# Head transfers in turn on one queue, a small fetch removed, shorter dataless matmuls, and late transfers by halves in a GEGLU kernel

## The chip, the core and the metric

The kernel runs on one core of a Trainium2 chip. The metric is device time in microseconds of that core, smaller is better; a kernel's time is the median of several executions. The engines are PE (TensorE; matmuls, and PEld for its weight loads), DVE (VectorE), ACT (ScalarE), POOL (GpSimd) and SP (SyncE). SP and ACT issue the transfers (DMAs) of this kernel, each on a queue of its own.

## The reference

```python
def setup_inputs():
    ...
    B, S, D, F = 32, 32, 1024, 3584
    return {
        "x": _w((lambda *s: _rng.normal(s) * 0.05)(B, S, D)),
        "w_gate": _w((lambda *s: _rng.normal(s) * 0.05)(D, F)),
        "w_up": _w((lambda *s: _rng.normal(s) * 0.05)(D, F)),
        "w_down": _w((lambda *s: _rng.normal(s) * 0.05)(F, D)),
    }

def reference(x, w_gate, w_up, w_down):
    return (_gelu(x @ w_gate) * (x @ w_up)) @ w_down
```

All tensors are bf16; `_gelu` is the tanh form.

## The kernel before

The 1024 tokens are two blocks of 512 (NB); D is 8 tiles of 128 (DT), F is 28 (FT). The kernel computes both layers with one level of a Winograd scheme: each product of 2 by 2 blocks takes seven block products in place of eight.

In the first layer the weights are the left matrix: a11 and a12 are the lower and upper four D tiles of `w_gate`, a21 and a22 those of `w_up`. The right matrix is x transposed: b11 and b21 are the lower and upper D tiles of token block 0, b12 and b22 those of block 1. t1 to t4 are sums of the b's (VectorE), s1 to s4 sums of the a's (mostly GpSimd). F runs in 14 chunks of two tiles (loop at L364).

Of the seven products, a12 times b21 needs no sums. For the first 24 F tiles it is done ahead, in the head of the kernel, and kept in fp32 (`ahead`). This is done in six groups of four F tiles (`group_ahead`, L293, `product_ahead`, L282); group i reads the tile `a12_ahead[i]` (a12a for groups 0 and 1, a12b for 2 to 5), which `load_ahead(i, k0, k1)` (L209) fills for the D tiles k0 to k1 of a12. These are "the kept gate rows".

Head of the kernel, L195 to L361, is ordered by hand (`manual_schedule`): each engine runs its instructions in the order of the code. x comes in two ways: for the first two D tiles of b21 as plain rows (`load_nat` into x_nat, L196), transposed on PE (`transposed`, L260) and copied by VectorE into b21; for all else by a transposing DMA (`load_xT`, L216). Before the first data, PE runs six dataless matmuls of 512 columns on a constant tile (NWARM, L255). PE then does group 0 for D tile 0 by halves of the tokens, the transposes of D tile 1, the rest of group 0's first two D tiles (matmuls of 256 columns), group 1's first two D tiles (L333, matmuls of 512 columns), the last two D tiles of both groups (L335), groups 2 to 4, the first product of chunk 0 (b11), and group 5.

The framework gives each transfer one of eight completion semaphores in turn. A transfer adds 16 to it when it has landed. A transfer that is given a semaphore whose earlier transfer may still be under way has to wait for that one's landing before it is issued.

Lines that the steps below touch: SP's first transfers at L203 to L243; ACT's three at L207 (the small fetch `probe`, 16 rows of 8 bytes that nothing reads), L223 (second x_nat) and L226 (group 1's first two D tiles); `gelu(ident...)` at L252, whose activation makes ACT load its table; the sums `t1` (L345, needs b11 and b12), `t2` (L351, needs b22), `b22r` (L352), `t3` (L354).

Of the kernel before, what the change touches and what calls it, by code (L numbers as in the profile page):

```python
# [8 lines left out]
ACT = mybir.ActivationFunctionType  # L9
# [4 lines left out]
def kernel(  # L14
# [20 lines left out]
    nc = tc.nc  # L35
    P = nc.NUM_PARTITIONS
    fp32 = mybir.dt.float32
    f32r = mybir.dt.float32r
    bf16 = mybir.dt.bfloat16
# [7 lines left out]
    NB = 512  # L47
    assert N == 2 * NB and D == 2 * NB and F % (4 * P) == 0
    DT, FT = D // P, F // P
    KD = DT // 2  # L50
# [4 lines left out]
    KQ = DT // 4  # L55
    HF = FT // 2
    MT = NB // P
    NWARM = 6
    KB = 4
    QF = HF // 2  # L60
    batches = [(0, KB), (KB, QF), (QF, QF + KB), (QF + KB, HF)]
# [2 lines left out]
    wg_r = w_gate.rearrange("(dt dp) f -> dp dt f", dp=P)  # L64
# [8 lines left out]
    xpool = one.enter_context(tc.tile_pool(name="x", bufs=1))  # L73
    ework = one.enter_context(tc.tile_pool(name="ework", bufs=2))
# [32 lines left out]
    def acc(tag):  # L107
        return ps1.tile([P, NB], fp32, name=f"ps{tag}", tag=tag, bufs=BANKS[tag])
# [18 lines left out]
    def alloc_w(ci, which):  # L127
        w_tiles[ci, which] = wpool.tile(
            [P, DT, FC * P], bf16, name=("wg", "wu")[which], tag=("wg", "wu")[which], bufs=(3, 2)[which]
        )  # L130

    def load_w(eng, ci, which, d0, d1):
        f0 = ci * FC * P
        src = (wg_r, wu_r)[which]
        eng.dma_start(out=w_tiles[ci, which][:, d0:d1, :], in_=src[:, d0:d1, f0 : f0 + FC * P])

    def load_w_all(ci, which):

        alloc_w(ci, which)
        if (ci, which) != (NCH - 1, 0):  # L140
            load_w(nc.sync, ci, which, 0, KD if which == 0 and a12_stays(ci) else DT)
            return


        for d0 in (0, KD):
            load_w(nc.sync, ci, which, d0, d0 + KD)

    def a12_stays(ci):
        return chunks[ci][-1] < 2 * KB
# [37 lines left out]
    ones_w = nc.const_aps.tensor(1.0, [P, P], bf16)  # L187
    ones_m = nc.const_aps.tensor(1.0, [P, NB], bf16)
    ident = xpool.tile([P, P], bf16, name="ident")
    make_identity(nc, ident)  # L190
    NB_P = NB // P
# [3 lines left out]
    with tc.manual_schedule():  # L195
        def load_nat(eng, dt, p0, p1):  # L196
            eng.dma_start(  # L197
                out=x_nat[:, p0:p1, dt * P : (dt + 1) * P],
                in_=xf[p0 * P : p1 * P, (KD + dt) * P : (KD + dt + 1) * P].rearrange("(b p) d -> p b d", p=P),
            )  # L200
# [1 line left out]
        assert KQ == 2  # L202
        load_nat(nc.sync, 0, 0, NB_P)  # L203


        probe = xpool.tile([P // 8, KQ, 2], bf16, name="probe")
        nc.scalar.dma_start(out=probe, in_=wg_r[::8, KD : KD + KQ, :2])  # L207

        def load_ahead(i, k0, k1, eng=nc.sync):  # L209
            f0 = i * KB  # L210
            eng.dma_start(
                out=a12_ahead[i][:, k0:k1, :],
                in_=wg_r[:, KD + k0 : KD + k1, f0 * P : (f0 + KB) * P],
            )

        def load_xT(nb, d0, d1):  # L216
            t = ((b11, b12), (b21, b22))[d0 // KD][nb]
            nc.sync.dma_start_transpose(
                out=t[:, d0 % KD : (d1 - 1) % KD + 1, :], in_=xf[nb * NB : (nb + 1) * NB, d0 * P : d1 * P]
            )  # L220

        load_ahead(0, 0, 1)
        load_nat(nc.scalar, 1, 0, NB_P)  # L223
        load_ahead(0, 1, 2)
        load_xT(0, KD + KQ, DT)
        load_ahead(1, 0, KQ, nc.scalar)  # L226
        a12_ahead += [spool.tile([P, KD, KB * P], bf16, name="a12b", tag=t) for t in ("s2", "s4", "s1", "s3")]
        for i in (0, 1):
            load_ahead(i, KQ, KD)
# [5 lines left out]
        load_halves(3)  # L235
        for which in (1, 0):
            load_w_all(0, which)
        load_ahead(4, 0, KD)
        load_xT(0, 0, KD)
        load_xT(1, 0, KD)  # L240
        load_ahead(5, 0, KD)
        load_xT(1, KD, DT)
        for which in (1, 0):  # L243
            load_w_all(1, which)

        def gelu(src, tag, bufs):
            h = ework.tile([P, NB], bf16, name=tag, tag=tag, bufs=bufs)[:, : src.shape[-1]]
            nc.scalar.activation(h, src, ACT.Gelu_apprx_tanh)  # L248
            return h


        gelu(ident[:, :1], "h0", 6)  # L252

        warm_ps = acc("A")
        for _ in range(NWARM):  # L255
            nc.tensor.matmul(warm_ps, lhsT=ones_w, rhs=ones_m, start=True, stop=True)

        tps = [[ps1.tile([P, HALF * P], bf16, name="tp", tag="A", bufs=BANKS["A"]) for _ in range(2)] for _ in range(KQ)]

        def transposed(dt):  # L260
            for half, tp in enumerate(tps[dt]):
                p0 = half * HALF
                for b in range(HALF):
                    nc.tensor.transpose(  # L264
                        tp[:, b * P : (b + 1) * P], x_nat[:, p0 + b, dt * P : (dt + 1) * P], ident
                    )
                nc.vector.tensor_copy(b21[:, dt, p0 * P : (p0 + HALF) * P], tp)

        transposed(0)

        def prod(ps, lhs, rhs, start):
            for k in range(KD):
                nc.tensor.matmul(  # L273
                    ps,
                    lhsT=lhs[:, k, :],
                    rhs=rhs[:, k, :],
                    start=(start and k == 0),
                    stop=(k == KD - 1),
                    skip_group_check=True,
                )  # L280
# [30 lines left out]
        def first_product(ft):  # L311
            psa = acc("A")
            prod(psa, quads(*chunk_of(ft))[0], b11, True)
            if ft < NAHEAD:
                return psa, gelu(added(ahead_at[ft], psa), "h0", 6)
            return psa, snap(psa, "sn1", 4)
# [34 lines left out]
        tt(t2, b22, t1, SUB)  # L351
        group_ahead(5, "CCAA", between=lambda: nc.scalar.copy(b22r, b22))  # L352
        begun = {ft: (psa, gelu(c, "h0", 6)) for ft, (psa, c) in begun.items()}
        tt(t3, b22, b12, SUB)  # L354
        next(chunk0)
# [8 lines left out]
        for ci in range(NCH):  # L364
# [8 lines left out]
            sn5, sn2, h1, h0 = [], [], [], []  # L373
# [17 lines left out]
            if fts[-1] < NAHEAD:  # L391
                h0 = first
# [226 lines left out]
```

## Time and profile before

| | us |
|---|---|
| median of 3 runs | 273.55 (273.33 to 275.83) |
| span of the profiled execution | 272.0 |
| PE busy | 267.1 (98%) |
| VectorE, ScalarE, GpSimd busy | 201.2, 116.1, 119.3 |
| data read, written | 31.72 MB, 2.10 MB |

The profile is one execution; the span runs from its first to its last instruction, and the time of a run also holds what lies around the span. Times in rows are microseconds from the span's start unless marked ns. A row such as `a<-b` names what is written and what is read; L284 is line 284 of the kernel. An engine followed by q (SPq, ACTq) is that engine's queue issuing a transfer: the length is that of the issue, not of the transfer.

PE's first stretch, in order of time (start, length, instruction, the idle time ahead of it and what ended it):

```profile
0.78 2.72 PE L256 MATMUL psA<-const-bfloat16-1.0 128*128 128x512 bf16 x6 [0.78 <-PEq L603]
...
3.30 0.62 PE L264 MATMUL tp<-ident,x_nat 128*128 128x128 bf16 x4
4.31 0.61 PE L284 MATMUL psC<-b,a12a 128*128 128x256 bf16 x2 [0.39 <-DMA a12a<-in_w_gate_dram]
```

### The profile page before, as it was taken

Reading aid. Unit: us, or ns where it says so; the run is one execution under the profiler, and the core shown is the slowest. Engines: PE = TensorE matmul, PEld = TensorE weight load, DVE = VectorE, ACT = ScalarE, POOL = GpSimd, SP = SyncE. Lnnn points to the kernel's source line nnn. Section 1 sums busy time; section 2 is a strip of 40 time slices with the busy share of each in tenths; the row PEclk is TensorE's granted clock in tenths of the full one; section 3 lists DMA queues with packets and bytes.
Section 4 is the critical chain, followed back from the end, with each engine's and each line's share of the span. In section 5 each row is a group of like instructions: output and inputs, shape, how many; then the busy total and the mean of one; then the engine's idle time right before and its main releaser. Section 6 shows DMA issues by size and latency. Waiting matters only on the chain.

```text
span 272.0 us, 3399 instructions
## 1 busy us (share of the span) xinstructions
PE 267.1 (98%) x1199; PEld 193.4 (71%) x1212; DVE 201.2 (74%) x205; ACT 116.1 (43%) x189; POOL 119.3 (44%) x60
## 2 busy tenths in 40 slices
PE   8999999999999999999999999999999999999995
PEld 4444776886787688688688687764458888888884
DVE  1448998886976876876787458569999999997721
ACT  2335865545644643645636535434000307770000
POOL 1090099976995994994995978000000000000000
PEclk9999999999999999999999999999999999999999
DMA  7999130504505505415234290005981437855111
GB/s 174 323 227 281 39 99 17 158 25 130 154 2 154 154 4 154 128 27 157 69 88 118 50 319 17 0 2 182 356 273 60 158 112 253 276 187 174 54 61 58
DMA packets 56048, 35.86 MB, mean 132 GB/s; under 512 B 9824, under 2 KB 56032, under 8 KB 56032
## 3 DMA queue, kind: packets, MB, share of 16 engines
q1 hardware_dynamic: 52736, 33.17, 42.6%
q10 hardware_dynamic: 3296, 2.49, 2.9%
q8 instruction: 9, 0.15, 0.2%
q14 instruction: 7, 0.06, 0.1%
HBM read 31.72 MB, written 2.10 MB: 124 GB/s over the span
## 4 chain that ended last, share of the span: by engine, by line
PE 97%; DMA 1%; issue 0%; SPq 0%; DVE 0%
PE psA L273 38%; PE psA L425 24%; PE psC L273 19%; PE psC L425 7%; PE psA L284 5%; PE psC L284 3%; PE psC L588 1%; DMA a12a<-in_w_gate_dram 1%; SPq L197 0%; PE tp L264 0%; DVE o_last L589 0%
## 5 line engine op out<-in xcount | busy, mean ns | idle before, releaser
L273 PE MATMUL psA<-t,s 128*128 128x512 f32 x224 | 57.2, 397 | 0.0
L248 ACT ACTIVATE h<-c 128x512 bf16<-128x512 f32 x56 | 34.6, 631 | 41.6 <-DVE c L303 41.6
L273 PEld LDWEIGHTS psA<-t,s 128*128 128x128 f32 x224 | 42.1, 188 | 9.5
L170 POOL TENSOR_TENSOR s<-wu 128x1024 fp32r<-128x1024 bf16 x13 | 28.8, 2215 | 32.9 <-DMA wu<-in_w_up_dram 27.9
L171 POOL TENSOR_TENSOR s<-s,wg 128x1024 fp32r<-128x1024 f32 x14 | 31.7, 2263 | 15.0 <-DVE s L170 14.0
L173 POOL TENSOR_TENSOR s<-wg,wu 128x1024 fp32r<-128x1024 bf16 x13 | 28.4, 2188 | 0.0
L273 PE MATMUL psA<-b,wg 128*128 128x512 bf16 x119 | 27.8, 379 | 0.6
L273 PE MATMUL psA<-t,a22r 128*128 128x512 f32 x112 | 27.9, 391 | 0.0
L273 PE MATMUL psC<-t,s 128*128 128x512 f32 x112 | 27.9, 391 | 0.0
L273 PE MATMUL psC<-b22r,s 128*128 128x512 f32 x112 | 27.6, 389 | 0.0
L303 DVE TENSOR_TENSOR c<-sn,psA 128x512 f32<-128x512 f32 x32 | 21.8, 682 | 6.7 <-PE psA L273 5.7
L308 ACT COPY sn<-psC 128x512 f32<-128x512 f32 x28 | 16.4, 590 | 20.9 <-PE psC L273 15.2
L273 PEld LDWEIGHTS psC<-t,s 128*128 128x128 f32 x112 | 21.0, 188 | 4.5
L273 PEld LDWEIGHTS psA<-t,a22r 128*128 128x128 f32 x112 | 21.0, 188 | 4.5
L273 PEld LDWEIGHTS psC<-b22r,s 128*128 128x128 f32 x112 | 21.0, 188 | 4.4
L303 DVE TENSOR_TENSOR c<-sn,psC 128x512 f32<-128x512 f32 x28 | 19.2, 688 | 6.5 <-PE psC L273 6.5
L273 PEld LDWEIGHTS <-wg 128*128 128x128 bf16 x128 | 11.8, 98 | 15.3 <-issue 2.4
L172 POOL TENSOR_TENSOR s<-wg,s 128x1024 fp32r<-128x1024 bf16 x10 | 21.6, 2158 | 0.8
L402 DVE TENSOR_TENSOR lo<-c,h 128x512 bf16<-128x512 f32 x14 | 20.4, 1459 | 0.9
L308 ACT COPY sn<-psA 128x512 f32<-128x512 f32 x32 | 18.4, 592 | 6.1 <-PE psA L273 6.0
L303 DVE TENSOR_TENSOR c<-ahead,psA 128x512 f32<-128x512 f32 x24 | 16.4, 687 | 4.0 <-PE psA L273 2.4
L321 DVE TENSOR_TENSOR hi<-h,psA 128x512 bf16<-128x512 bf16 x14 | 9.6, 688 | 12.4 <-PE psA L273 12.4
(85 smaller groups left out, 381.0 us busy)
## 6 DMA issues: line engine op xcount, KB each, us to landing
wu<-in_w_up_dram SPq DMA_DIRECT2D x14, 512.0 KB, 4.0
wdb<-in_w_down_dram SPq DMA_DIRECT2D x12, 512.0 KB, 4.9
wg<-in_w_gate_dram SPq DMA_DIRECT2D x9, 512.0 KB, 5.2
wdb<-in_w_down_dram SPq DMA_DIRECT2D x12, 384.0 KB, 4.5
v<-in_w_down_dram SPq DMA_DIRECT2D x4, 512.0 KB, 6.4
out_dram<-o_sb ACTq DMA_DIRECT2D x15, 128.0 KB, 1.7
wg<-in_w_gate_dram SPq DMA_DIRECT2D x6, 256.0 KB, 4.6
v<-in_w_down_dram SPq DMA_DIRECT2D x4, 384.0 KB, 7.5
```

Source lines behind the costliest of these rows:

```text
L170: yield engs[0].tensor_tensor(s1, a21, a22, ADD)
L171: yield engs[1].tensor_tensor(s2, s1, a11, SUB)
L172: yield engs[2].tensor_tensor(s4, a12, s2, SUB)
L173: yield engs[3].tensor_tensor(s3, a11, a21, SUB)
L248: nc.scalar.activation(h, src, ACT.Gelu_apprx_tanh)
L273: nc.tensor.matmul(ps, lhsT=lhs[:, k, :], rhs=rhs[:, k, :], start=(start and k == 0), stop=(k == KD - 1), skip_group_check=True,)
L284: nc.tensor.matmul(ps[:, cols], lhsT=a12_ahead[i][:, k, j * P : (j + 1) * P], rhs=b21[:, k, cols], start=(k == 0 and not cols.start), stop ...
L303: tt(t, s, ps, ADD)
L308: nc.scalar.copy(t, ps)
L321: tt(g_of(ft)[:, :NB], h0, psa, MUL)
L402: tt(g_of(ft)[:, NB:], added(sn5[fl], psa[fl]), h1[fl], MUL)
L425: nc.tensor.matmul(banks[m], lhsT=lhs(k)[:, m * P : (m + 1) * P], rhs=rhs(k), start=(start and k == 0), stop=(k == HF - 1), skip_group_che ...
```

## The change

- SP issues the head's first four transfers in turn: first x_nat, group 0's D tile 0, second x_nat (before on ACT's queue), group 0's D tile 1.
- The small fetch `probe` is gone.
- `gelu(ident...)`, with the table load, now stands ahead of ACT's one remaining transfer, group 1's first two D tiles.
- Five dataless matmuls in place of six, and two groups of two short ones (128 columns, `fill`): one ahead of the transposes of D tile 0, one behind them.
- The kept rows of groups 4 and 5 and the transposed loads of b11 and b12 go by halves (two D tiles) in turn; b22 goes by halves too, and chunk 1's gate rows stand ahead of b22, its up rows behind.

```diff
-    NWARM = 6
+    NWARM = 5
+    NFILL = 2
...
-        probe = xpool.tile([P // 8, KQ, 2], bf16, name="probe")
-        nc.scalar.dma_start(out=probe, in_=wg_r[::8, KD : KD + KQ, :2])
...
+        def gelu(src, tag, bufs):
+            h = ework.tile([P, NB], bf16, name=tag, tag=tag, bufs=bufs)[:, : src.shape[-1]]
+            nc.scalar.activation(h, src, ACT.Gelu_apprx_tanh)
+            return h
+
+
+        gelu(ident[:, :1], "h0", 6)
+
         load_ahead(0, 0, 1)
-        load_nat(nc.scalar, 1, 0, NB_P)
+        load_nat(nc.sync, 1, 0, NB_P)
         load_ahead(0, 1, 2)
+        load_ahead(1, 0, KQ, nc.scalar)
         load_xT(0, KD + KQ, DT)
-        load_ahead(1, 0, KQ, nc.scalar)
...
-        load_ahead(4, 0, KD)
-        load_xT(0, 0, KD)
-        load_xT(1, 0, KD)
-        load_ahead(5, 0, KD)
-        load_xT(1, KD, DT)
-        for which in (1, 0):
-            load_w_all(1, which)
-
-        def gelu(src, tag, bufs):
...
-        gelu(ident[:, :1], "h0", 6)
+        for i, nb in ((4, 0), (5, 1)):
+            for k in range(0, KD, KQ):
+                load_ahead(i, k, k + KQ)
+                load_xT(nb, k, k + KQ)
+        load_w_all(1, 0)
+        load_xT(1, KD, KD + KQ)
+        load_xT(1, KD + KQ, DT)
+        load_w_all(1, 1)
 
         warm_ps = acc("A")
         for _ in range(NWARM):
             nc.tensor.matmul(warm_ps, lhsT=ones_w, rhs=ones_m, start=True, stop=True)
+
+        def fill():
+            for _ in range(NFILL):
+                nc.tensor.matmul(warm_ps[:, :P], lhsT=ones_w, rhs=ones_w, start=True, stop=True)
+
+        fill()
...
         transposed(0)
+        fill()
```

The built programs differ in one more way that the diff does not spell out. These are ACT's first instructions with the semaphores they wait for, before and after:

```
L207 DMACopy probe<-in_w_gate_dram 16x2x2
L197 DMACopy x_nat<-in_x_dram 128x4x128
L211 DMACopy a12a<-in_w_gate_dram 128x2x512
L248 LoadActFuncSet
L248 Activation h0<-ident 128x1 [waits Pool]
```

```
L221 LoadActFuncSet
L221 Activation h0<-ident 128x1 [waits Pool]
L208 DMACopy a12a<-in_w_gate_dram 128x2x512 [waits DMAHW4 >= 16]
```

DMAHW4 is the semaphore that the first transposing DMA of x (b21's last two D tiles, on SP) raises by 16 when it has landed. ACT's load raises it by another 16, and PE's first weight load of group 1 waits for that.

More of the change, by code (lines that the diff above doesn't have):

```diff
@@ L237 @@
             load_w_all(0, which)
-        load_ahead(4, 0, KD)
-        load_xT(0, 0, KD)
-        load_xT(1, 0, KD)
-        load_ahead(5, 0, KD)
-        load_xT(1, KD, DT)
-        for which in (1, 0):
-            load_w_all(1, which)
-        def gelu(src, tag, bufs):
-            h = ework.tile([P, NB], bf16, name=tag, tag=tag, bufs=bufs)[:, : src.shape[-1]]
-            nc.scalar.activation(h, src, ACT.Gelu_apprx_tanh)
-            return h
-        gelu(ident[:, :1], "h0", 6)
+        for i, nb in ((4, 0), (5, 1)):
[6 more added lines that the diff above has]
+        load_w_all(1, 1)
         warm_ps = acc("A")
```

## The prediction

> **What bounds the kernel now.** I read the page's chain first: does any engine but PE carry it, and where does it leave PE?
>
> ```profile
> PE 97%; DMA 1%; issue 0%; SPq 0%; DVE 0%
> ```
>
> PE carries 97%, so what is not PE's own work is a few us. The same chain in order of time, for the first 60 us:
>
> ```profile
> 1.25 3.02 DMA a12a<-in_w_gate_dram
> ...
> 4.31 0.61 PE psC L284 x2
> 4.92 0.43 PE psA L284 x2
> ...
> 6.10 0.22 PE psA L284 x2
> ...
> 7.11 1.95 PE psA L284 x10
> ```
>
> The columns are start, length and what. PE's chain begins with the landing at 4.27 (1.25 + 3.02) of the first gate row tile, and from there PE follows PE to the end. So the end moves one for one with any time that PE loses or gains after 4.31. The row at 7.11 is where group 1 begins, the first product that reads gate tile a12a of the second group; I use it as the mark. The rows also show pace: two 256-column matmuls took 0.43 at 4.92 and 0.22 from 6.10. PE thus ran at half its later pace until about 6.0, 5.3 us after its first matmul at 0.78, although the granted clock in the rows stands at 1.00 throughout; the six dataless matmuls took 2.72.
>
> Next the two engines that issue the head's transfers, in order of time, SyncE and then ScalarE (start, length, instruction):
>
> ```profile
> 0.74 0.45 SPq L197 DMA_DIRECT2D x_nat<-in_x_dram  x1
> 1.25 1.03 SPq L211 DMA_DIRECT2D a12a<-in_w_gate_dram  x2
> 2.32 1.34 SPq L218 DMA_TRANSPOSE b<-in_x_dram  x1
> ...
> 19.21 3.65 SPq L218 DMA_TRANSPOSE b<-in_x_dram  x1
> ```
>
> ```profile
> 1.73 0.53 ACTq L211 DMA_DIRECT2D a12a<-in_w_gate_dram  x1
> 2.29 1.28 ACT L248 ACT_TABLE_LOAD   x1 [2.29 <-issue]
> 3.59 0.21 ACT L248 ACTIVATE h<-ident 128x1 bf16<-128x1 bf16 x1
> ```
>
> Issues on SP follow each other 0.51 apart (1.25 - 0.74). ScalarE issues group 1's first gate rows at 1.73, waiting for nothing. Last the DMA issues of these moments (size, us from issue to landing):
>
> ```profile
> x_nat<-in_x_dram SPq DMA_DIRECT2D x1, 128.0 KB, 2.5
> x_nat<-in_x_dram ACTq DMA_DIRECT2D x1, 128.0 KB, 3.2
> a12a<-in_w_gate_dram ACTq DMA_DIRECT2D x1, 256.0 KB, 4.6
> ```
>
> ```profile
> b<-in_x_dram SPq DMA_TRANSPOSE x1, 4.9
> ```
>
> Group 1's first rows landed at 1.73 + 4.6 = 6.3, 0.8 before their use at 7.11. The first transposed load of x (the one at 2.32) landed at 2.32 + 4.9 = 7.2.
>
> **The change part by part.**
>
> *The held load.* In the built program ScalarE's load of group 1's first gate rows now carries a wait: the semaphore that the first transposed load of x raises must have reached 16, that load's landing. Before, it had its own semaphore and no wait; the two loads share one now because ScalarE's turn comes after its table load and activation, when SP's transfers have gone once round the eight semaphores. So this load cannot be issued before x's transposed load has landed, and PE waits for it at the mark. Behind it in ScalarE's queue stand only the copies of finished groups, which need PE anyway.
>
> When does the transposed load land? SP issues one more transfer ahead of it, so it starts at 2.32 + 0.51 = 2.83 and, at 1.34, is issued by 4.17. Low end: the transposed load at 19.21 was issued by 22.86 and landed 5.7 after its start, at 24.9, that is 2.05 after its issue; 4.17 + 2.05 = 6.2. High end: the 4.9 of before from its start, 2.83 + 4.9 = 7.7. I take 6.6, nearer the low end: in the run of before 384 KB of ScalarE's transfers moved among SP's in these microseconds (128 KB landing at 4.4, 256 KB at 6.3), and these are gone from ahead of it.
>
> How long does the held load then take? Low end 2.5, the first x_nat, which had the DMA engines nearly to itself at half the size. High end 4.6, the same load of before, which stood behind 128 KB on its own queue. At its new time SP's queue is full: the windows show 344 to 352 GB/s from 7 to 10. ScalarE's 128 KB took 3.2 beside SP's loads; another 128 KB at half of 344 GB/s is 131/172 = 0.76, or 3.96; the faster engines of that later moment (344 against 203 to 232 GB/s at 2 to 4 us) take some off. I take 3.7.
>
> PE passes the mark at 6.6 + 0.1 + 3.7 = 10.4 in place of 7.11 (0.1 for the two hand-overs; PE began 0.05 after the landing at 4.27). That is 3.3 us later. Ends: 6.2 + 0.1 + 2.5 = 8.8, 1.7 later; 7.7 + 0.1 + 4.6 = 12.4, 5.3 later. Everything PE needs next (the later gate rows of groups 0 and 1, group 2) is issued on SP between 4.2 and 7 and takes 4.2 to 5.3 as before, so no second wait follows.
>
> *First four transfers on SP, no small fetch, shorter dataless matmuls.* Five long at 0.43 (2.15) and two short ones (a quarter of the columns, 0.11 each) end at 0.78 + 2.15 + 0.22 = 3.15, before the first x_nat (0.74 + 2.5 = 3.24). The two fills after the transposes take 0.22 while VectorE copies (its first copy ran from 3.75 to 4.04), so they delay nothing. Gate row 0 no longer shares the engines with ScalarE's transfers; it landed at 4.27 and PE can't start before the copy at 4.04: a gain of 0 to 0.26. Gate row 1 is issued at 2.27 in place of 1.76 and takes 2.5 to 4.4 (the row of before), landing at 4.8 to 6.7; PE waited 0.25 for it at 6.28: from a gain of 0.25 to a loss of 0.4. Together I take a gain of 0.4, and PE at the mark at 6.7. All of it is swallowed by the wait until 10.4; it counts only if the held load is in time. The dropped fetch frees 0.48 of ScalarE's issue time (0.73 to 1.21), also before the wait.
>
> *The clock behind the stall.* PE would stand from 6.7 to 10.4, 3.7 us. The longest PE idle that the trace shows after its start is below 1 us, so no row tells whether the pace halves again. Bounds: 0, or half of the 5.3 us of the first start, 2.65. That first start held some 1.3 us of waits (0.71 for x_nat, 0.39 and 0.25 for gate rows), so 4.0 busy us at half pace, a loss of 2.0, is what I take if it does.
>
> The Trainium skill speaks against the change here: by "TensorE: Matmul & The Clock Gate", Part 1, the half-rate state returns after an idle window of about 3.4 us, and a busy window lifts it. The trace agrees with the second half (half pace first, full pace from about 6.0) and shows nothing of the first. By that rule a 3.7 us gap would about suffice where the free-running window happens to fit into it, and an estimate from the page's window is 3.4/2 = 1.7 us lost.
>
> *Late kept rows and x's transposes by halves.* Six transposed halves and four gate halves replace three and two whole ones, same bytes. SP is 0.51 later there, and the held load's 256 KB (0.75 at 350 GB/s) now moves among them. First users in the run of before: group 4 at about 19.3, b11 at 22.7, group 5 at 24.4; landings then 15.9, 19.5 (10.30 + 9.2), 23.0 (17.34 + 5.7). Group 4's second half now stands behind one transposed half (256 KB, 0.9 at 290 GB/s): 15.9 + 0.5 + 0.75 + 0.9 = 18.1, in time. b12 stands behind group 5: from 21.2 to at most 21.2 + 0.5 + 0.75 + 1.5 = 24.0; VectorE's t1 and t2 (2.3 each) with two sums (1.5) between end at 30.1, where PE wanted t2 at 29.74. With PE 3.3 later that is hidden; without, it costs up to 0.4. The second chunk's up rows swap places with gate rows: landed 27.3, wanted at 32.98. Nothing.
>
> The sum: 0 + 3.3 + 0 = 3.3. The profiled span is 272.0; 1.55 lie around it up to the median of 273.55. So 275.3 in the span and 276.85 in time.
>
> **The rivals.**
>
> *The clock closes in the stall.* The 2.0 come on top: 278.85. For it: the first start; against: the gap is short. The span from 6.7 to 10.4 may also just miss.
>
> *Not slower by 1%: the two landings are quick.* The transposed load lands at 6.2 and the held load in about 3.0, since ScalarE's own queue is otherwise empty: PE passes the mark at 9.2, 2.1 later, 275.6. It decides when the sum of both landings puts the mark before 9.85 (7.11 + 2.74). For it: x_nat's 2.5; against: SP's full queue.
>
> *The load is not held in effect.* If the wait were met early, ScalarE would issue at about 2.3 (0.74 + 1.28 + 0.21 and a hand-over) and land at 6.9 at the latest: the head's 0.4 show, 273.15; with full pace reached 3 us sooner, another 0.9 (half of 4.31 to 6.10). Against: the wait is for the full 16.
>
> **How the numbers follow.** Stall with an open clock 0.45; stall and closed clock 0.32; quick landings 0.17; not held 0.06. The likeliest gives 276.85, rounded to 276.9. Its own ends of 1.7 and 5.3 are 275.25 and 278.85. The range is 275.2 to 279.4: it leaves out the unheld case, the slowest fifth of the closed clock and the quickest of the quick landings, about 0.15. One per cent is 2.74 us, about what a measurement of this kernel tells from no change. Of the first case 0.36 lies above it, of the closed clock all, of the quick one 0.02: slower 0.70, same 0.29, faster 0.01.
>
> **What would show it.** ScalarE's timeline: its one DMA issue at 6 to 7.7, not at 2. The waits: PE's weight load idle over 2 us before the first 512-column matmul of a12a, released by DMA a12a. The chain: that transfer in place of PE before the mark. The pace of the rows after the mark, 0.22 or 0.43 for 512 columns, tells the clock. I am wrong if PE passes the mark before 9, if a later tile of a12a or a12b ends a second wait, or if PE waits on b11, t1 or t2 between 22 and 35.

## The result and the profile after

| | before | after |
|---|---|---|
| median, us | 273.94 (6 runs, 273.33 to 275.83) | 282.48 (6 runs, 281.93 to 283.42) |
| ratio, 95% interval | | 1.030 (1.027 to 1.033) |
| span of the profiled execution | 272.0 | 280.3 |

The change makes the kernel 3% slower, 8.5 us; the two profiled spans differ by 8.3. From the page after, the row of the granted clock (40 slices of 7 us) and the chain by engine:

```profile
PEclk9779999999999999999999999999999999999999
...
PE 94%; DMA 4%; SPq 1%; DVE 0%; issue 0%
```

Transfers now hold 4% of the chain in place of 1%, and the second and third slice have a lower clock. The chain after in order of time (start, length, what):

```profile
2.79 3.58 DMA b<-in_x_dram
6.37 0.02 issue
6.39 6.54 DMA a12a<-in_w_gate_dram
12.93 0.05 issue
12.97 3.59 PE psA L289 x8
16.56 1.31 PE psC L289 x4
17.87 2.59 PE psA L289 x12
20.46 1.73 PE psC L289 x8
```

This is the forecast mechanism: x's transposed load lands at 6.37, 0.02 later ScalarE issues its load, and PE passes the mark when that has landed. But it takes 6.54. For the mark of before, the prediction's row at 7.11 has to be read more closely: its ten matmuls are group 0's last two of 256 columns and group 1's first eight of 512 (at full pace eight of 512 take 1.73, two of 256 take 0.22, together 1.95), so group 1 began at 7.33. The mark moves from 7.33 to 12.97, 5.64 later. These are the rows of group 2 and of the last product before, and of the last product after:

```profile
12.51 1.73 PE psC L284 x8
...
266.01 3.09 PE psC L588 x28
```

```profile
273.97 3.09 PE psC L593 x28
```

Group 2 began at 12.51; it begins at 20.46, 7.95 later. So another 2.31 are lost between the mark and group 2: eight matmuls of 512 columns take 3.59 at 12.97 and twelve take 2.59 at 17.87, 0.45 and 0.22 each. From there to the end nothing more is lost on PE (the last product begins 7.96 later); the remaining 0.3 lies behind the last addition (2.5 to the end of the span before, 2.8 after), and the last store lands 1.6 after its issue in both. ScalarE's queue and engine, and the load's landing:

```profile
0.73 1.28 ACT L221 ACT_TABLE_LOAD   x1 [0.73 <-PEq L608]
2.02 0.21 ACT L221 ACTIVATE h<-ident 128x1 bf16<-128x1 bf16 x1
6.39 0.43 ACTq L208 DMA_DIRECT2D a12a<-in_w_gate_dram  x1
```

```profile
a12a<-in_w_gate_dram ACTq DMA_DIRECT2D x1, 256.0 KB, 6.5
```

ScalarE was free at 2.23 and issued at 6.39. The windows show the clock (the columns are the window, its length, busy time and instructions of PE, PEld, DVE, ACT, POOL, granted clock, DMA share, GB/s):

```profile
9.00:10.00 1.00, 0.00 (x0) 0.00 (x0) 0.00 (x0) 0.00 (x0) 0.00 (x0) 1.00 0.94 297
10.00:11.00 1.00, 0.00 (x0) 0.00 (x0) 0.00 (x0) 0.00 (x0) 0.00 (x0) 0.76 0.99 318
11.00:12.00 1.00, 0.00 (x0) 0.00 (x0) 0.00 (x0) 0.00 (x0) 0.00 (x0) 0.50 1.09 365
...
16.00:17.00 1.00, 1.00 (x4) 0.38 (x3) 0.00 (x0) 0.00 (x0) 1.00 (x1) 0.50 0.84 190
17.00:18.00 1.00, 1.00 (x5) 0.42 (x4) 0.09 (x1) 0.55 (x1) 0.92 (x2) 0.83 1.13 314
```

PE stops at about 6.35. The granted clock falls to half at 10.5 (0.76 over that window), 4.2 after PE stopped, and is full again at 17.3 (0.83). PE works at half pace from 12.97 to 17.3; half of 4.3 is 2.2, nearly all of the 2.31 above.

### The profile page after: what moved, and what is told of

It reads as the page before. It is cut to its first block, busy times and chain, and to the rows that moved or that the text cites. A ratio compares the mean times of both kernels' runs of the same rounds, so it can differ in the third digit from the quotient of the medians.

```text
span 280.3 us, 3425 instructions
## 1 busy us (share of the span) xinstructions
PE 269.6 (96%) x1215; PEld 193.6 (69%) x1215; DVE 202.2 (72%) x205; ACT 115.9 (41%) x189; POOL 119.4 (43%) x60
## 4 chain that ended last, share of the span: by engine, by line
PE 94%; DMA 4%; SPq 1%; DVE 0%; issue 0%
PE psA L278 37%; PE psA L430 24%; PE psC L278 18%; PE psC L430 7%; PE psA L289 5%; DMA a12a<-in_w_gate_dram 2%; PE psC L289 2%; DMA b<-in_x_dram 1%; PE psC L593 1%; SPq L208 0%; SPq L198 0%; DVE o_last L594 0%
## 5 line engine op out<-in xcount | busy, mean ns | idle before, releaser
L278 PE MATMUL psA<-b,wg 128*128 128x512 bf16 x128 | 29.4, 380 | 0.0
L407 DVE TENSOR_TENSOR lo<-c,h 128x512 bf16<-128x512 f32 x14 | 21.1, 1508 | 0.9
```

The costliest lines, as they stand in the source:

```text
L278: nc.tensor.matmul(ps, lhsT=lhs[:, k, :], rhs=rhs[:, k, :], start=(start and k == 0), stop=(k == KD - 1), skip_group_check=True,)
L407: tt(g_of(ft)[:, NB:], added(sn5[fl], psa[fl]), h1[fl], MUL)
```

## The experiments

The theory after the result: the held load is the whole loss, through its wait (ready at 2.3, issued at 6.39), its long way to landing (6.54), and the clock that closed meanwhile. Rivals: one of the other parts costs something, or the half pace has another cause.

**Its own semaphore.** A small copy by ScalarE into the first a12b tile makes SP's next load wait for it; in the program built so, the held load is given a semaphore that nothing used before, and waits for nothing.

```diff
+        nc.scalar.copy(a12_ahead[2][:, 0, :1], ident[:, :1])
         load_halves(2)
```

> Hold theory (the whole loss comes from ScalarE's load waiting for x's first transposed load, and what follows from that): the load is issued at about 2.3, lands by 6.9, PE passes the mark (first 512-column matmul of a12a) at 6.4 to 7.1 in place of 12.97, the clock stays open, and the time is 273.0 to 274.2 (ratio to the kernel before 0.996 to 1.002). Rival (moving the second x_nat to SP, the short dataless matmuls or the late halves cost something of their own): the wait is gone and the time stays over 275.5.

Measured: 274.96, ratio 1.005 (1.002 to 1.008), so by the ratios (1.030 and 1.005) 6.9 of the loss are gone; but the time is 0.8 above the expected range, between the two theories. From the chain of this run:

```profile
1.24 3.37 DMA a12a<-in_w_gate_dram
4.61 0.05 issue
4.66 0.60 PE psC L290 x2
...
7.97 0.39 PE psC L290 x2
8.36 1.95 PE psA L290 x10
...
13.76 1.73 PE psC L290 x8
```

The load was issued at 1.35, while the activation table was still loading, and its 256 KB now moved with gate row 0, which landed at 4.61 (3.6 in the changed kernel). PE, moreover, kept half pace until about 8.2 (0.4 for two matmuls of 256 columns), where the kernel before had full pace from 6.0. The wait is no longer there, but PE passes the mark at 8.6, not at 6.4 to 7.1. In this one execution what remains (group 2 begins at 13.76, 1.25 later than before) is the later gate row and the longer half pace.

**The activation alone.** The kernel before with one line moved: the activation ahead of ScalarE's third transfer. The second x_nat, the small fetch, the long dataless matmuls and the late loads are as before. In the built program this transfer waits for x's transposed load.

```diff
+        gelu(ident[:, :1], "h0", 6)
         load_ahead(1, 0, KQ, nc.scalar)
...
-        gelu(ident[:, :1], "h0", 6)
```

> The kernel before, with one part of the change: the activation moved ahead of ScalarE's third transfer. In the built program that transfer now waits for x's first transposed load, as in the changed kernel. Hold theory: issued at 6.0 to 7.3, landing 4.9 to 6.6 later, mark at 11.0 to 13.5, time 279.5 to 283. Rival (the loss needs x_nat on SP's queue or the short matmuls): under 276.

Measured: 281.65, ratio 1.027 (1.022 to 1.031). Its chain:

```profile
2.32 3.85 DMA b<-in_x_dram
6.17 0.02 issue
6.19 6.14 DMA a12a<-in_w_gate_dram
12.33 0.05 issue
12.38 3.60 PE psA L284 x8
```

All as expected: the same wait, the same long landing (6.14), the same half pace at the mark. Moving the activation is enough for 2.7% of loss, and this interval overlaps that of the whole change (1.027 to 1.033): the transfers moved to SP and the fills are not needed for it.

**The load's way.** Two runs hold the load in the same manner, by a copy that reads the transposed load's result, and hold SP's later loads back by a copy into their tile: with nothing of a12b ahead ("no backlog"), and with one a12b tile (two loads) ahead ("half of the backlog"). This is the edit of the first; in the second `load_halves(2)` stands ahead of the held load and the last copy goes into `a12_ahead[3]`.

```diff
-        load_ahead(1, 0, KQ, nc.scalar)
...
+        held = (1, 0, KQ, nc.scalar)
...
+        nc.scalar.copy(late_x, b21[:, KQ, :1])
+        load_ahead(*held)
+        nc.scalar.copy(a12_ahead[2][:, 0, :1], ident[:, :1])
         load_halves(2)
```

> Queue theory (ScalarE's transfer moves only after everything that SP has issued before it): the load is again issued at about 6.4 to 6.6, with only the two gate tiles of groups 0 and 1 ahead of it, some 400 KB left: 667 KB with its own at 310 GB/s is 2.2, plus about 1.3 to the first packet, so it lands 3.2 to 3.8 after its issue, the mark is at 9.7 to 10.4, and the time 277.0 to 279.5 (the clock may close or not). Rival (the load is slow of itself on ScalarE's queue at that moment, or shares evenly with SP's): it lands 6 or more after its issue, and the time stays at 281.5 to 283.

> Queue theory: two tiles of a12b more stand ahead than in the run with no backlog, 524 KB or 1.7 at 310 GB/s: it lands 4.9 to 5.5 after its issue, the mark is at 11.4 to 12.0, the time 279.5 to 281.5. Even sharing: the transfers issued ahead of it cost only half their bytes, 4.0 to 4.5 after its issue.

Measured: 280.37 (ratio 1.022, 1.016 to 1.028) and 280.80 (1.028, 1.021 to 1.035); landing 4.87 and 4.65 after the issue at 6.40 and 6.39:

```profile
6.40 4.87 DMA a12a<-in_w_gate_dram
```

```profile
6.39 4.65 DMA a12a<-in_w_gate_dram
```

Both beat the 6.54, but neither theory holds as it stood: the two do not differ as the queue theory wanted. With no backlog the landing missed its range of 3.2 to 3.8 by 1.1 and the time its range by 0.9; with half of the backlog the 4.65 lies between the ranges of the two theories. The transfers by queue tell why (q1 is SP's queue, q10 ScalarE's; packets, MB, share of the engines). The changed kernel from 8 to 9, and from 10 to 11:

```profile
q1 hardware_dynamic: 326, 0.32, 98.6%
```

```profile
q1 hardware_dynamic: 170, 0.16, 54.9%
q10 hardware_dynamic: 158, 0.16, 44.0%
```

From 6.4 to 9 no packet of ScalarE's load moved, 33 moved from 9 to 10, most from 10 to 11. With no backlog the first 30 moved from 7 to 8; with half of it 3 from 8 to 9, and most from 9 to 10. The first packet moved about 1.1, 2.4 and 3.0 after the issue with no, half and the whole backlog. The start goes by what SP had issued earlier: by 6.4 SP had issued 1.31 MB with no backlog and 0.92 had moved (the windows' GB/s summed), 0.39 left, 1.3 at 310 GB/s; with half of the backlog 0.9 left, 2.8; in the changed kernel 0.9 to 1.2, 3.0 to 3.8, depending on how much of its next load, just being issued, counts. The end, however, goes by what SP issues later: with no backlog SP's a12b loads follow at 7.12 and share the engines. The clock closed in both runs; with no backlog this window has it at 0.57 (1.00 up to 9.14, then 0.50), and PE's last matmul had ended at 6.92:

```profile
9.00:10.00 1.00, 0.00 (x0) 0.00 (x0) 0.00 (x0) 0.00 (x0) 0.00 (x0) 0.57 0.96 282
```

**Quiet.** The same, but SP's a12b loads wait until the held load has landed (the copy into their tile reads the held load's tile).

```diff
-        nc.scalar.copy(a12_ahead[2][:, 0, :1], ident[:, :1])
+        nc.scalar.copy(a12_ahead[2][:, 0, :1], a12_ahead[1][:, 0, :1])
```

> As the run with no backlog, but SP's a12b loads start only when the held load has landed, so that behind it nothing moves: it has two gate tiles (about 400 KB left) ahead of it and none beside it. If the tail of 3.5 between its first packet and its landing with no backlog came from SP's later loads, it lands 3.0 to 3.8 after its issue; if it is the load's own, 4.5 or more again.

```profile
7.10 2.93 DMA a12a<-in_w_gate_dram
10.03 0.05 issue
10.08 3.48 PE psA L292 x8
```

It landed 2.93 after its issue, just under the expected 3.0 to 3.8, so the tail did come from SP's later loads. (x's transposed load landed 0.7 later here, at 7.07. This is a single execution, of 279.29.) Of the 6.54, then, 2.9 is the load with little ahead and nothing behind it, and 3.6 is SP's other traffic, ahead of it and beside it.

**A busy stall.** The changed kernel with 28 dataless matmuls ahead of the mark.

```diff
+        for _ in range(28):
+            nc.tensor.matmul(ps[1][0], lhsT=ones_w, rhs=ones_m, start=True, stop=True)
         for j in range(KB):
             product_ahead(ps[1][j], 1, j, 0, KQ)
```

> 28 dataless matmuls of 512 columns (6.0 at full pace) stand in the stall; nothing else changes, the mark stays at 12.9 to 13.1. Clock theory (PE's idle of 6.6 closed the clock, at a cost of 2.1): the ten matmuls behind the mark run 0.22 apart in place of 0.43, the granted clock stays 1.00, and the time is 280.0 to 280.8. Rival (the half pace has another cause, such as the full DMA engines): they still run 0.43 apart, and the time stays at 282 to 283.

Measured: 280.25, ratio 1.023 (1.018 to 1.027), by the ratios 2.1 less than the changed kernel.

```profile
6.45 6.51 DMA a12a<-in_w_gate_dram
12.96 0.05 issue
13.01 1.90 PE psA L289 x8
...
18.36 1.73 PE psC L289 x8
```

The mark stands where it was, the eight matmuls behind it take 1.90 in place of 3.59, and the granted clock stays at 1.00 from 6 to 18. From the mark to group 2 it takes 5.35 here (13.01 to 18.36) and 7.49 in the changed kernel, so the clock cost 2.14; the 0.17 that is left of the 2.31 is there with the open clock too. The transfers are the same in both, so the half pace was the clock, and the clock closed for want of work.

**Repaired, and the other parts.** Three runs issue the held load as SP's fifth transfer: with the rest of the change as it is; with the late part as before; and with six long dataless matmuls and no short ones. The edit that all three have:

```diff
-        load_ahead(1, 0, KQ, nc.scalar)
+        load_ahead(1, 0, KQ)
```

> The held load goes on SP as its fifth transfer, ahead of x's first transposed load, and waits for nothing. Hold theory: issued at 2.8, landed at 5.8 to 6.6; gate row 0 lands at 3.6 as in the changed kernel, PE passes the mark at 6.4 to 7.1, and the time is 272.8 to 274.0, within 0.3% of the kernel before. Rival (the rest of the change costs something): 275 or more, as the run with its own semaphore (274.96).

> As the run with the load as SP's fifth transfer, but with the late kept rows and x's transposes whole and in the order of before. If the halves do nothing, as predicted, the two runs agree within 0.3%; if the halves cost the third of a per cent that the run with its own semaphore left, this one is 0.8 or more faster; if they gain, it is slower, with PE waiting on b11, t1 or t2 between 20 and 35.

> As the run with the load as SP's fifth transfer, with six long dataless matmuls and no short ones, as before. If the short ones cost the 0.36% that the repaired kernel still stands above the kernel before, the time falls by 0.8 to 1.0, to 274.2; if they do nothing or help the clock open early, it stays at 275.2 or rises.

And three parts alone on the kernel before: the short dataless matmuls, the late halves, the small fetch taken out.

> The kernel before with the short dataless matmuls alone (five long, two and two short). My prediction's step says within 0.3 of the kernel before, with a gain of up to 0.9 where the clock opens earlier; if the short ones are what is left of the loss, it is 0.8 to 1.0 slower.

> The kernel before with the late rows and x's transposes by halves alone. My prediction's step: t2 may be late by up to 0.4, so 0 to 0.4 slower; if the halves are what is left of the loss, 0.8 to 1.0 slower.

> The kernel before without the small fetch: ScalarE's two loads are issued at 0.73 and 1.21, half a microsecond earlier. If its issue time is all it costs, the head moves little: the second x_nat and group 1's rows land 0.3 to 0.5 earlier, gate rows of group 0 a little later for it, the time within 0.4 of the kernel before. If the fetch helps the transfers behind it in a way no row shows, 0.8 or more slower.

| run | median, us | ratio (95%) |
|---|---|---|
| load as SP's fifth | 275.21 | 1.0036 (1.0010 to 1.0062) |
| same, late part as before | 274.90 | 1.0022 (0.9992 to 1.0053) |
| same, no short matmuls | 275.25 | 1.0035 (1.0008 to 1.0062) |
| before, short matmuls alone | 273.76 | 0.9995 (0.9967 to 1.0022) |
| before, late halves alone | 274.14 | 0.9988 (0.9958 to 1.0019) |
| before, no small fetch | 273.82 | 0.9983 (0.9956 to 1.0011) |

By the ratios the repair takes back 7.3. It missed its range (272.8 to 274.0) all the same and came out at the rival's 275: with the hold gone, 0.36% (0.10 to 0.62) is still lost. None of the three parts tried alone on the kernel before costs anything beyond its interval, and the repaired kernel's two variants differ from it by 0.3 and 0.04 only. The repaired kernel does not gain what its head gains: group 2 begins at 12.28 in it and at 12.51 in the kernel before, and yet its last product begins 0.24 later. VectorE's row for t1 in the repaired kernel shows where:

```profile
23.49 2.29 DVE L350 TENSOR_TENSOR t<-b,b 128x2048 fp32r<-128x2048 bf16 x1 [3.57 <-DMA b<-in_x_dram]
```

t1 waits for b12, which stands behind group 5's rows, until 23.49 (21.29 before), VectorE is behind from there, and PE loses some 0.3 at 41.6, where four matmuls take 1.20 in place of 0.9. With the late part as before PE waits 0.48 for group 5's rows at 24.2 instead, and its last product begins at 266.24, as late as here. The rest of the 0.36% was not found. The order of table load and transfers on ScalarE without a hold, and the second x_nat on SP alone, were not tried. No run here beats the kernel before by more than its interval.

## Why the prediction was wrong

The direction, the mechanism and the place were right; the time lay outside the range. The step that failed is the landing of the held load, put at 3.7 and at most 4.6: it took 6.54. With that term alone put right the sum is 273.55 + 5.64 = 279.2, inside the top of the range; the closed clock, which stood in a rival, adds 2.14 and carries it out. Step by step:

- *x's transposed load lands at 6.6.* Right: 6.37, nearer still to the low end of 6.2.
- *The held load takes 3.7, at most 4.6.* This is the term that failed: 6.54. I let it share SP's traffic by half ("another 128 KB at half of 344 GB/s") and closed the range with the same load in the run of before. That row was no upper bound: it was issued at 1.73, when SP had issued two or three small transfers, and this one stands behind some 1 MB that SP had issued earlier. The row to bound it by was in the trace: SP's own loads of a12b, wu and wg, issued at these moments into the same engines, took 4.6 to 7.1 to land (a12b, issued from 4.8 to 6.8, 4.6 to 5.4; wu, issued at 6.88, 6.7; wg, issued at 7.40, 7.1). The runs show 2.93 with SP quiet and 6.1 to 6.5 with its full queue.
- *The clock.* I put its closing in a rival of 0.32, because the stall I expected (3.7) was short. The stall was 6.6 and the clock closed. It closed in shorter stalls too: in the quiet run, with a stall of 3.3, 3.4 after PE's last matmul (0.1 after PE had begun again), in the run with half of the backlog 2.5 after it, and with no backlog and with the activation alone 2.2 after it. The stall of 3.7 that I forecast was therefore no reason against it. The price of 2.0 was right (2.14), in part by luck: it was taken from the first start, and what a closed spell costs goes by how much of it PE works in, here 4.3 of 6.8. The Trainium skill's rule ("TensorE: Matmul & The Clock Gate", Part 1) is that half rate comes back after an idle window of about 3.4 us. The runs agree in so far as the clock closed in all five profiled stalls (3.3 to 6.6) in which PE was not kept busy; but a closing 2.2 after PE's last matmul shows that 3.4 of idle behind it are not needed. Nor does each such stall close it: one execution with no backlog (278.45) has a mean granted clock of 0.999, where its profiled execution has 0.988.
- *Head's gain of 0.4, swallowed.* Swallowed, yes; it was 1.0: PE began group 0 at 4.00 in place of 4.31, gate row 1 landed at 5.24 (2.24 + 3.0) in place of 6.16 (1.76 + 4.4), and group 0's first two D tiles ended at 6.35 in place of 7.33. Part of this is luck: the clock opened at about 3.7 here and at 6.0 in the profile of before.
- *The mark at 7.11.* Misread by 0.22, as said above: group 1 began at 7.33, so the forecast mark of 10.4 would have been 3.1 later and not 3.3.
- *Late halves: nothing with the stall, up to 0.4 without.* Right: nothing in the kernel before alone, and about 0.3 of waiting for VectorE in the repaired kernel.
- *No second wait follows.* Right.

The sum with the sizes measured: 5.64 + 2.31 + 0.3 = 8.25, and the spans differ by 8.3.

## What to carry to other kernels

A framework that hands out completion semaphores in turn turns a change of order into a wait that no line of the source shows: after any move of a transfer, read in the built program what it waits for. Price a late transfer by the transfers issued at that moment on all queues, not by the same transfer at an earlier and emptier one. A stall of PE is to be priced with the clock that can close in it (2.1 us here), or filled with dataless matmuls.

## What the runs showed of the hardware

- ScalarE's transfer did not share the engines evenly with SP's: for 2.6 us (6.4 to 9) not one of its packets moved while SP's queue moved 0.77 MB (0.14 + 0.31 + 0.32). Once it had begun, later transfers of SP shared with it.
- The closed spells of the clock have two lengths: 6.8 us in the changed kernel (10.5 to 17.3), with no backlog (9.1 to 16.0), half of it (9.8 to 16.6) and the activation alone (9.8 to 16.6), and 3.4 in the quiet run (10.2 to 13.6). The time from PE's first full pace to the closing is near 3.4 or 6.8 too (3.7 to 10.5 in the changed kernel, about 5.7 to 9.1 with no backlog). The closing came 2.2 to 4.2 after PE's last matmul. So in these traces the clock seems to change only at steps of 3.4 us that do not begin where PE stops; no run was made to test this.
- The moment when PE first reaches full pace differs much between executions with nearly the same first work: about 3.7 in the changed kernel, 6.0 before, 8.2 in the run with its own semaphore. At half pace in between, 4.5 us later cost some 2.2 us of PE's time (an estimate). Single executions of the kernel before differ by up to 3 us in their span; whether this is the reason was not tested.
- A transfer can be issued by ScalarE while its activation table loads: issued at 1.35, table load from 0.74 to 2.02, in the run with its own semaphore.
